# A spectral filter and a SoLU feed-forward layer on one core: the first entry's spectrum by channel halves, and its filter's sums on TensorE

## The chip, the cores and the metric

The kernel runs on one core of one Trainium2 chip. The metric is the device time of one execution in microseconds (us), the median over the runs. One more execution is recorded by the hardware profiler; its rows, groups and timelines are called the profile and the trace here.

Names: TensorE is PE (its weight loads PEld), VectorE is DVE, ScalarE is ACT, GpSimd is POOL, SyncE is SP. SP, ACT and POOL also issue DMAs, each on a queue of its own. A line such as L605 is line 605 of the kernel before.

## The reference

```python
X = np.fft.rfft(x, axis=1)                    # x: 8 entries, 3136 tokens, 256 channels, float32
Y = X * (filt_r + 1j * filt_i)[None, :, :]    # 1569 frequencies, 256 channels
y = np.fft.irfft(Y, n=3136, axis=1)           # bridge: (8 * 3136, 256) = 25088 tokens
h = y @ w_in                                  # w_in: 256 x 1024
e = np.exp(h - h.max(-1)); sm = e / (e.sum(-1) + 1e-9)
solu = h * sm
ln = (solu - mean(solu)) / sqrt(var(solu) + 1e-6) * g_ln
out = ln @ w_out                              # w_out: 1024 x 256
```

The weights lie in DRAM as 64-bit floats and are brought to 32 bits on the chip.

## The kernel before

Each entry's transform over 3136 = 49 x 64 tokens is done in two matrix products each way. The first step (`pa`) multiplies 49 rows by a table of 25 residues; the second (`pb`, in `forward`) multiplies, for each of 13 pairs of residues, two blocks of 64 rows by tables of cosines and sines and gives the spectrum, real part in one PSUM bank and imaginary part in another. The filter multiplies the spectrum; `inverse` (`pc`) goes back through the transposed tables; `back` (`py`) makes the tokens, which lie in `y` with channels on the partitions.

Entries 1 to 7 pass through DRAM between the steps (`d1`, `d2`) and are woven into a long loop over blocks of 128 tokens (`step`), which does the feed-forward layer: `product` (the `m` tiles), the maximum, exponential and mean, a turn by 32 x 32 blocks, `project` (the `o` tiles). Products are done by Strassen's scheme with 7 products for 8. Each step's place is written in lists; all orders on all engines are fixed when the program is built.

Entry 0 is done before the loop, in the opening, and stays on the chip. The change lies there. The opening's order is the order of the statements (`manual_schedule`), for each engine:

- x's 98 rows are fetched in 8 pieces of 4 + 4 columns (plain and mirrored); row 49 (the last of each half) comes apart, in four parts of 16 columns (`fetch_last`). The mirrored half of piece 0 and the four parts are issued by ACT, all else by SP. Then follow, on SP, tables and filters in three groups, half of w_in, constants, pieces of entry 1 and w_out.
- Each DMA of SP and ACT raises one of eight completion counters when it lands. The build hands the counters out in turn, and a DMA that gets a counter waits for the counter's earlier holder.
- VectorE brings two of the four raw quarters of w_in to 32 bits (`load_float64`, 9 instructions each).
- TensorE does 6 products that only warm it (`warm`), then `pa` (L605), which ACT evacuates (the last half piece VectorE); then rows of products that only keep it busy (`idle`) and the transposed tables (`tables_back`, L509).
- VectorE turns all of `pairs_x` in four quarters of 64 channels (`turn_rows`, L625), in place.
- Seven units of two pairs (the last has one, with one residue), 256 channels each: `forward` (8 products of 64 x 64 by 256 columns), four products with the filter on VectorE (L341, L342), a difference and a sum on POOL (L343), `inverse` (8 products), two evacuations on ACT (L359).
- `turn_rows` again; then the first step of three pieces of entry 1 (L245) with their stores, the other conversions, the sums of w_in's quarters, and `back` for all 8 pieces and both halves of the channels (L413).

PSUM has eight banks. Six of them, `ps_h`, go round in three pairs; two, `ps_t`, serve `pc`, the tables and `py`.

Of the kernel before, what the change touches and what calls it, by code (L numbers as in the profile page):

```python
# [9 lines left out]
FP32 = mybir.dt.float32  # L10
# [40 lines left out]
SHRINK = 1.0 / (32 * DFF)  # L51

# [51 lines left out]
def kernel(  # L104
# [327 lines left out]
    with ExitStack() as st:  # L432
        fpool = pool("fp", 1, stack=st)
        pools = {name: pool(name + "0", bufs, stack=st)
                 for name, bufs in (("r", 1), ("p", 3))}
        rows_x = pools["r"].tile([P, NH, C], FP32, name="x_0", tag="r")
        pairs_x = rows_x.rearrange("p m c -> p (m c)").rearrange("p (a c t) -> p a c t", c=C, t=2)
        wpool = pool("wp", 4, stack=st)
        ps_h = pool("ps_h", 3, PSUM, stack=st)

        def load_float64(dst, raw, power):


            lo, hi = raw[:, :, 0], raw[:, :, 1]
            frac, rest = dst.bitcast(I32), lo.bitcast(FP32)
            ts, tt, stt = (nc.vector.tensor_scalar, nc.vector.tensor_tensor,
                           nc.vector.scalar_tensor_tensor)
            return [
                lambda: ts(out=lo, in0=lo, scalar1=8, scalar2=None, op0=ALU.logical_shift_right),
                lambda: ts(out=power, in0=hi, scalar1=20, scalar2=0x7FF, op0=ALU.logical_shift_right,  # L450
                           op1=ALU.bitwise_and),
                lambda: ts(out=power, in0=power, scalar1=896.0, scalar2=0.0, op0=ALU.subtract,
                           op1=ALU.max),
                lambda: ts(out=power, in0=power, scalar1=255.0, scalar2=2.0 ** 23, op0=ALU.min,
                           op1=ALU.mult),
                lambda: ts(out=frac, in0=hi, scalar1=0xFFFFF, scalar2=3, op0=ALU.bitwise_and,
                           op1=ALU.logical_shift_left),
                lambda: stt(out=power, in0=hi, scalar=-2 ** 31, in1=power, op0=ALU.bitwise_and,
                            op1=ALU.bitwise_xor),
                lambda: tt(out=frac, in0=frac, in1=power, op=ALU.bitwise_or),  # L460
                lambda: stt(out=rest, in0=lo, scalar=2.0 ** -44, in1=power.bitcast(FP32), op0=ALU.mult,
                            op1=ALU.mult),
                lambda: tt(out=dst, in0=dst, in1=rest, op=ALU.add)]
# [6 lines left out]

        filters, tables = {}, {}


# [8 lines left out]
        def fetch_second(rows):  # L482
            for i in rows:
                second.fetch_x(i, [lambda out, in_: nc.sync.dma_start(out=out, in_=in_)] * 2,
                               spare_piece(i))

# [13 lines left out]
        one = fpool.tile([P, P], FP32, name="one", tag="one")  # L500

        def tables_back(i0, n):

            de = tables[i0][0]
            for first in range(0, n, 4):
                size = min(4, n - first)
                ps = ps_t.tile([P, 4, P], FP32, name=f"back_{i0}_{first}", tag="t")
                for v in range(size):
                    nc.tensor.matmul(out=ps[:, v], lhsT=de[:, first + v, 0].rearrange("p u q -> p (u q)"),  # L509
                                     rhs=one, start=True, stop=True)  # L510
                nc.scalar.copy(out=de[:, first:first + size, 1].rearrange("p i u q -> p i (u q)"),
                               in_=ps[:, 0:size])

# [5 lines left out]

        def resident(held):  # L520
            def find(sp, u):
                i, pairs = sp.units[u]
                tile, at = held[i]
                return tile[:, at:at + pairs]
            return find

        sp = Spectrum(0, pools, resident(filters), resident(tables))
# [6 lines left out]
        def halves(name):  # L534
            ps = ps_h.tile([P, 2, 512], FP32, name=name, tag="h")
            return [ps[:, u, :].rearrange("p (v c) -> p v c", c=C) for u in range(2)]

        def fetch_x(h, n0, n, r0, rows, dma):

            first, step = (n0, C) if h == 0 else (N2 - 1 - n0, -C)  # L540
            to = NR - 1 if r0 else (N1 - 1) * h
            dma(out=rows_x[to:to + rows, n0:n0 + n],
                in_=bass.AP(tensor=x.tensor, offset=x[0].offset + r0 * N2 * C + first * C,
                            ap=[[N2 * C, rows], [step, n], [1, C]]))
# [5 lines left out]
        def fetch_last(h, n0, dma):  # L550

            n = NH // 2
            first = n0 if h == 0 else N2 - n0 - n
            dma(out=rows_x[NR - 1 - h:NR - h, n0:n0 + n][:, ::1 - 2 * h],
                in_=bass.AP(tensor=x.tensor, offset=x[0].offset + ((N1 - 1) * N2 + first) * C,
                            ap=[[N2 * C, 1], [C, n], [1, C]]))

        for i in range(pieces):
            if i:
                fetch_x(0, NCH * i, NCH, 0, N1 - 1, nc.sync.dma_start)  # L560
            fetch_x(1, NCH * i, NCH, 0, N1 - 1, nc.sync.dma_start if i else nc.scalar.dma_start)
            if i == 0:
                fetch_last(1, 0, nc.scalar.dma_start)
                fetch_x(0, 0, NCH, 0, N1 - 1, nc.sync.dma_start)
                for h, n0 in ((0, 0), (0, NH // 2), (1, NH // 2)):
                    fetch_last(h, n0, nc.scalar.dma_start)
            if i in (2, 5):
                begin((0, 2)[i // 3], nc.sync.dma_start)
        nc.scalar.copy(out=small_consts[:, 5:6], in_=small_consts[:, 0:1])
        nc.gpsimd.dma_start(out=one, in_=one_dram)  # L570
        for i0, n in ((0, 4), (4, 4), (8, NP - 8)):
            for load in (load_tables, load_filters):
                load(i0, n, nc.sync.dma_start)
        begin(1, nc.sync.dma_start)
        begin(3, nc.sync.dma_start)
        nc.sync.dma_start(out=wf_t, in_=wf_dram)
        nc.sync.dma_start(out=wi_t, in_=wi_dram)
        nc.sync.dma_start(out=g_sb, in_=moe_g_ln.rearrange("(k p) -> p k", p=P))
        fetch_second(range(EARLY))
# [19 lines left out]
        for j in range(6):  # L599
            nc.tensor.matmul(out=ps_t.tile([P, P], FP32, name=f"warm_{j}", tag="t"), lhsT=wf0_t, rhs=wf0_t,  # L600
                             start=True, stop=True)
# [12 lines left out]
        def idle(out):  # L614

            nc.tensor.matmul(out=out, lhsT=one, rhs=one, start=True, stop=True)

        def idle_row(count, name):
            for j in range(count):
                idle(ps_h.tile([P, P], FP32, name=f"{name}_{j}", tag="h"))  # L620

        def turn_rows():
            for first in range(0, C, 64):
                part = pairs_x[:, :, first:first + 64].rearrange("p a c t -> p c a t")
                nc.vector.transpose(out=part, in_=part)  # L625

        for i0, n in ((0, 4), (4, 4)):
            idle_row(12, f"idle_{i0}")
            tables_back(i0, n)
        turn_rows()  # L630

        def start(i):
            i0, n = sp.units[i]
            sp.t2s[i] = pairs_x[:, i0:i0 + n]
            sp.fetch_filter(i)
            sp.fetch_de(i)
            sp.forward(i, halves(f"pb_0_{i}"))

        units = len(sp.units)

        order = [*range(units // 2), units - 1, *range(units // 2, units - 1)]
        for i in order[:2]:
            start(i)
        tables_back(8, NP - 8)
        early_weights = [op for ops in zip(conversion(1), conversion(3)) for op in ops]
        for at, i in enumerate(order):
            if at + 2 < units:
                start(order[at + 2])
            ended = at == units - 1
            sp.multiply(i, 0, nc.gpsimd.tensor_tensor)  # L650
            sp.multiply(i, 1, (nc.vector if ended else nc.gpsimd).tensor_tensor)
            if ended:
                for op in early_weights[:5]:
                    op()
            pss = [ps_t.tile([P, 2, C], FP32, name=f"pc_0_{i}_{u}", tag="t") for u in range(2)]
            i0, n = sp.units[i]
            sp.inverse(i, pss, pairs_x[:, i0:i0 + n], ended)
        turn_rows()
        for i in range(EARLY):
            for u in range(2):  # L660
                second.first(i, (u,), ps_t.tile([P, 2, C], FP32, name=f"pa_1_{i}_{u}", tag="t").rearrange(
                    "p a c -> p (a c)").rearrange("p (o n) -> p o n", o=1), nc.scalar.copy,
                    second.xs[i][0:NK, 2 * u:2 * u + 2, :])
                second.store_first(i, 2 * u, nc.gpsimd.dma_start)
        for ch in range(pieces):
            t4s[0, ch] = pairs_x[:, 2 * ch:2 * ch + 2]
        for op in early_weights[5:]:
            op()
        weight_sums(w_in_sb)
        for cb in range(KD):  # L670
            for ch in range(pieces):
                back(0, ch, cb, nc.scalar.copy)
# [557 lines left out]
```

## Time and profile before

| what | value |
|---|---|
| runs | 1584.10, 1579.68, 1583.47 us; median 1583.47 |
| span of the profiled execution | 1578.8 us |
| PE busy in the span | 1537.3 us (97%) |
| DVE, ACT, POOL busy | 1261.8, 923.8, 1142.2 us |
| granted TensorE clock, mean | 0.995 |
| first `pa`, first `pb`, first `py`, first `m` | 9.05, 36.75, 63.54, 78.67 us |

The profiled execution's own time is given as its span, from the first to the last instruction; what lies around the span is not in it. The last row is the start of each stage of the opening on TensorE. In the timelines a row gives start, duration, engine, line and operation, written tile and read tiles, count, and the idle time before it with what ended it. ACTq and SPq are DMA issues on these engines' queues. TensorE does a float32 product in two passes, and the trace counts passes.

### The profile page before, as it was taken

Reading aid. Unit: us, or ns where it says so; the run is one execution under the profiler, and the core shown is the slowest. Engines: PE = TensorE matmul, PEld = TensorE weight load, DVE = VectorE, ACT = ScalarE, POOL = GpSimd, SP = SyncE. Lnnn points to the kernel's source line nnn. Section 1 sums busy time; section 2 is a strip of 40 time slices with the busy share of each in tenths; the row PEclk is TensorE's granted clock in tenths of the full one; section 3 lists DMA queues with packets and bytes.
Section 4 is the critical chain, followed back from the end, with each engine's and each line's share of the span. In section 5 each row is a group of like instructions: output and inputs, shape, how many; then the busy total and the mean of one; then the engine's idle time right before and its main releaser. Section 6 shows DMA issues by size and latency. Waiting matters only on the chain. (4 is left out here: it accounts for less than half of the span.)

```text
span 1578.8 us, 36696 instructions
## 1 busy us (share of the span) xinstructions
PE 1537.3 (97%) x12836; PEld 1062.9 (67%) x12836; DVE 1261.8 (80%) x2280; ACT 923.8 (59%) x1886; POOL 1142.2 (72%) x1327
## 2 busy tenths in 40 slices
PE   7988999999999999999999999999999999999997
PEld 4733666667666776667666776667677777777777
DVE  4978978997989788877988688977997777777773
ACT  2455665566556556665556656566556665666562
POOL 0447976787878677887779767886766767676665
PEclk9999999999999999999999999999999999999999
DMA  9758877877987688667886588766874545344444
GB/s 248 229 162 228 241 211 209 244 207 202 242 260 206 174 231 250 205 172 189 240 234 195 151 227 240 215 179 174 228 207 120 139 123 132 90 115 109 108 111 106
DMA packets 341756, 298.08 MB, mean 189 GB/s; under 512 B 28096, under 2 KB 311370, under 8 KB 341572
## 3 DMA queue, kind: packets, MB, share of 16 engines
q1 hardware_dynamic: 276898, 172.78, 41.3%
q0 software_dynamic: 30352, 89.66, 18.9%
q10 hardware_dynamic: 34324, 33.30, 7.2%
q8 instruction: 104, 1.70, 0.5%
q14 instruction: 78, 0.64, 0.1%
HBM read 118.02 MB, written 74.84 MB: 122 GB/s over the span
## 5 line engine op out<-in xcount | busy, mean ns | idle before, releaser
L937 PEld LDWEIGHTS o<-w_out_sb,solu_t 128*128 128x128 f32 x3136 | 382.0, 192 | 49.2 <-issue 43.5
L801 PE MATMUL m<-w_in_sb,s 128*128 128x512 f32 x784 | 398.8, 610 | 6.5 <-DVE nmax L825 4.3
L937 PE MATMUL o<-w_out_sb,solu_t 128*128 128x128 f32 x3136 | 401.3, 276 | 2.7 <-DVE ot L957 2.3
L937 PEld LDWEIGHTS o<-w_out_sb,u 128*128 128x128 f32 x2352 | 307.3, 192 | 138.5 <-issue 107.1
L801 PE MATMUL m<-w_in_sb,y 128*128 128x512 f32 x588 | 308.2, 607 | 5.6 <-DVE nmax L825 4.1
L937 PE MATMUL o<-w_out_sb,u 128*128 128x128 f32 x2352 | 310.7, 276 | 2.5 <-POOL u L780 1.9
L847 DVE SCALAR_TENSOR_TENSOR h<-e,h 128x1024 f32<-128x1024 f32 x196 | 306.8, 1565 | 0.0
L811 ACT COPY h<-m 128x512 f32<-128x512 f32 x294 | 173.2, 589 | 198.6 <-PE m L801 179.8
L953 ACT ACTIVATE ot<-o,rs_t 128x128 f32<-128x128 f32 x392 | 143.5, 367 | 246.9 <-PE o L937 244.6
L780 POOL TENSOR_TENSOR u<-solu_t 128x512 f32<-128x512 f32 x98 | 133.7, 1365 | 187.2 <-DMA solu_t<-turn 108.8
L825 DVE CUSTOM_DVE_ANT_0 h<-m,h 128x512 f32<-128x512 f32 x196 | 134.0, 684 | 166.1 <-ACT h L811 101.8
L855 ACT ACTIVATE h<-h,nmu 128x1024 f32<-128x1024 f32 x196 | 225.0, 1148 | 56.4 <-DVE turn L865 56.4
L865 DVE STREAM_TRANSPOSE turn<-h 128x1024 f32<-128x1024 f32 x196 | 243.1, 1240 | 3.5 <-DMA out_dram<-ot 0.3
L835 ACT ACTIVATE e<-h,nmax 128x1024 f32<-128x1024 f32 x196 | 225.3, 1150 | 9.6 <-DVE h L847 8.2
L780 POOL TENSOR_TENSOR u<-solu_t,u 128x512 f32<-128x512 f32 x98 | 137.9, 1408 | 93.3 <-PE o L937 92.8
L801 PEld LDWEIGHTS m<-w_in_sb,s 128*128 128x128 f32 x784 | 128.1, 191 | 92.8 <-issue 71.9
L957 DVE SCALAR_TENSOR_TENSOR ot<-o,rs_t,ot 128x128 f32<-128x128 f32 x299 | 103.7, 347 | 99.9 <-ACT ot L953 58.0
L780 POOL TENSOR_TENSOR u<-u,solu_t 128x512 f32<-128x512 f32 x98 | 162.2, 1655 | 15.3 <-PE o L937 7.1
L801 PEld LDWEIGHTS m<-w_in_sb,y 128*128 128x128 f32 x588 | 96.7, 191 | 101.9 <-issue 48.4
L780 POOL TENSOR_TENSOR solu_t<-solu_t,solu_t 128x512 f32<-128x512 f32 x98 | 155.3, 1585 | 0.9
L780 POOL TENSOR_TENSOR s<-y 128x128 f32<-128x128 f32 x196 | 103.7, 529 | 14.7 <-ACT y L417 14.3
L390 PEld LDWEIGHTS py<-wb_t,t 50*64 50x64 f32 x3584 | 57.8, 134 | 43.8 <-issue 17.9
(122 smaller groups left out, 1942.5 us busy)
## 6 DMA issues: line engine op xcount, KB each, us to landing
solu_t<-turn SPq DMA_DIRECT2D x780, 128.0 KB
out_dram<-ot SPq DMA_DIRECT2D x196, 128.0 KB
t<-d POOLq DMA_DIRECT2D x112, 200.0 KB, 6.6
d<-x POOLq DMA_DIRECT2D x100, 200.0 KB, 5.1
f<-f_dram POOLq DMA_DIRECT2D x39, 512.0 KB, 7.8
t<-d ACTq DMA_DIRECT2D x37, 512.0 KB
d<-g POOLq DMA_DIRECT2D x36, 512.0 KB, 5.2
x<-in_x_dram SPq DMA_DIRECT2D x112, 98.0 KB
```

Of the source, the lines that this page charges most:

```text
L390: nc.tensor.matmul(out=views[g][64 * h:64 * h + 64, cb, i, :], lhsT=t4[rows, i, c0:c0 + 64], rhs=wb_t[rows, 0:N1], start=True, stop=True)
L780: nc.gpsimd.tensor_tensor(out=out, in0=in0, in1=in1, op=op)
L801: nc.tensor.matmul(out=ms[j, bank], lhsT=lhsT, rhs=w_in_sb[:, w, :], start=m in (1, 2, 7), stop=True, skip_group_check=True)
L811: nc.scalar.copy(out=h_half(k, i), in_=ms[j, 0])
L825: nc.vector.tensor_tensor_reduce(out=h_half(k, i), in0=ms[j, bank], in1=h_half(*kept), scale=1.0, scalar=sofar, op0=ALU.add, op1=ALU.min, ...
L835: nc.scalar.activation(out=e, in_=hs[k], func=AFT.Exp, bias=nmaxs.pop(k)[:, 1:2], scale=-1.0, accum_out=esums[g][:, i:i + 1])
L847: nc.vector.scalar_tensor_tensor(out=solu, in0=e, scalar=SHRINK, in1=solu, op0=ALU.mult, op1=ALU.mult, accum_out=nmu)
L855: nc.scalar.activation(out=solu, in_=solu, func=AFT.Square, bias=nmu, scale=-float(DFF), accum_out=variances[g][:, i:i + 1])
L865: nc.vector.transpose(out=turns[g][:, :, i, :], in_=solus[k].rearrange("p (f j) -> p f j", j=32))
L937: nc.tensor.matmul(out=pos[p, bank], lhsT=lhs[:, f, :], rhs=w[:, f, :], start=f == 0 and (m in (1, 2, 7) or alone), stop=True, skip_group_ ...
L953: nc.scalar.activation(out=out_half(p, *to)[0], in_=pos[p, 0], func=AFT.Copy, scale=rs)
L957: nc.vector.scalar_tensor_tensor(out=ot, in0=pos[p, bank], scalar=rs, in1=out_half(p, *kept)[0], op0=ALU.mult, op1=ALU.add)
```

## The change

It replaces the second half of entry 0's opening.

- The last row of x comes in two whole transfers of 32 columns, issued by ACT ahead of all others; ACT's third transfer is the mirrored half of piece 0.
- The second DMA order: the pieces of entry 1 now stand before the other half of w_in.
- A conversion to 32 bits takes 8 instructions.
- 8 warm-up products for 6; 12 idle ones for 24, with one group of transposed tables between them and two groups placed later.
- Units have four pairs (the last one pair, one residue) and one half of the channels, eight in all. The turn is done by quarters: two before the first `forward`, the others between units; the turn back likewise.
- `multiply` forms four products and no sum: those of the real part on VectorE; those of the imaginary part on POOL from a copy (`held`) that ACT makes, for five units, and on VectorE for three.
- `inverse` adds the products on TensorE: for each pair, residue and part it does one matrix product with the table and one with the table or its negative (`minus`, made by ACT next to the transposed tables).
- Each of the three pieces of entry 1 is done whole, one between units of the second half, one after the next turn, one at the end; they use a `ps_h` pair.

```diff
-        for i in range(pieces):
-            if i:
-                fetch_x(0, NCH * i, NCH, 0, N1 - 1, nc.sync.dma_start)
-            fetch_x(1, NCH * i, NCH, 0, N1 - 1, nc.sync.dma_start if i else nc.scalar.dma_start)
-            if i == 0:
-                fetch_last(1, 0, nc.scalar.dma_start)
-                fetch_x(0, 0, NCH, 0, N1 - 1, nc.sync.dma_start)
-                for h, n0 in ((0, 0), (0, NH // 2), (1, NH // 2)):
-                    fetch_last(h, n0, nc.scalar.dma_start)
+        for h in range(2):
+            fetch_last(h, nc.scalar.dma_start)
+        for i in range(pieces):
+            fetch_x(0, NCH * i, NCH, nc.sync.dma_start)
+            fetch_x(1, NCH * i, NCH, nc.sync.dma_start if i else nc.scalar.dma_start)
...
+        nc.sync.dma_start(out=wf_t, in_=wf_dram)
+        fetch_second(range(EARLY))
         begin(1, nc.sync.dma_start)
         begin(3, nc.sync.dma_start)
-        nc.sync.dma_start(out=wf_t, in_=wf_dram)
...
-        for j in range(6):
+        for j in range(WARM):
...
+                nc.scalar.mul(minus[:, i0 + first:i0 + first + size], ps[:, 0:size, 0:NQ], -1.0)
...
+        def multiply(k, half, shared):
+            i0, n, residues = extent(k)
+            rows = slice(0, NQ * residues)
+            f, at = filters[i0]
+            f = f[rows, at:at + n, :, P * half:P * half + P]
+            re, im = (ps[rows, 0:n] for ps in spectra.pop((k, half)))
+            parts[k, half] = of_re, of_im = [
+                ppool.tile([P, 2, 4, P], FP32, name=f"p{kind}_0_{k}_{half}", tag=f"p{kind}") for kind in "ri"]
+            for part in range(2):
+                nc.vector.tensor_tensor(out=of_re[rows, part, 0:n], in0=re, in1=f[:, :, part], op=ALU.mult)
+            if shared:
+                held = ppool.tile([P, 4, P], FP32, name=f"im_0_{k}_{half}", tag="im", bufs=1)[rows, 0:n]
+                nc.scalar.copy(out=held, in_=im)
+            engine = nc.gpsimd if shared else nc.vector
+            for part in range(2):
+                engine.tensor_tensor(out=of_im[rows, part, 0:n], in0=held if shared else im,
+                                     in1=f[:, :, 1 - part], op=ALU.mult)
+
+        def inverse(k, half):
...
+            for r in range(2):
+                for u in range(residues):
+                    rows = slice(NQ * u, NQ * u + NQ)
+                    for v in range(n):
+                        there = de[rows, at + v, 1, r, :]
+                        for part, by in ((of_re, there), (of_im, there if r else minus[rows, i0 + v, :])):
+                            nc.tensor.matmul(out=pss[u][NQ * r:NQ * r + NQ, v, :], lhsT=by,
+                                             rhs=part[rows, r, v], start=part is of_re, stop=True,
+                                             skip_group_check=True)
+            for u in range(residues):
+                nc.scalar.copy(out=pairs_x[:, i0:i0 + n, P * half:P * half + P, u], in_=pss[u][:, 0:n])
...
+        idle_row(6, "idle_0")
+        tables_back(0, 4)
+        idle_row(6, "idle_1")
+        for n in range(2):
+            turn_quarter(n)
+        forward(0, 0)
+        turn_quarter(2)
+        forward(1, 0)
+        multiply(0, 0, True)
+        tables_back(4, 4)
+        inverse(0, 0)
+        turn_quarter(3)
+        multiply(1, 0, True)
+        forward(0, 1)
+        inverse(1, 0)
+        multiply(0, 1, False)
+        forward(2, 0)
+        tables_back(8, NP - 8)
+        inverse(0, 1)
+        forward(3, 0)
+        multiply(2, 0, True)
+        forward(1, 1)
+        multiply(3, 0, False)
+        inverse(2, 0)
+        inverse(3, 0)
+        multiply(1, 1, True)
+        forward(2, 1)
+        turn_quarter(0)
+        first_of_second(0)
+        inverse(1, 1)
+        multiply(2, 1, True)
+        forward(3, 1)
+        turn_quarter(1)
+        first_of_second(1)
+        multiply(3, 1, False)
+        inverse(2, 1)
+        inverse(3, 1)
+        first_of_second(2)
+        for n in range(2, 4):
+            turn_quarter(n)
+        for j in (1, 3):
+            for op in conversion(j):
+                op()
```

## Prediction

> **What bounds the kernel now.** I read the page first: span, the busy rows, the chain.
>
> ```profile
> span 1578.8 us, 36696 instructions
> PE   7988999999999999999999999999999999999997
> DVE  4978978997989788877988688977997777777773
> ```
>
> From about 160 us on TensorE is at 9 tenths or more in nearly every slice, and the change leaves that part alone. An edit to the opening therefore shifts the end by what it shifts the moment at which TensorE takes up the long loop. The next view is the table by stretches, cut at the borders of the opening's stages (columns: stretch, PE, PEld, DVE, ACT, POOL busy, granted clock, DMA share, GB/s).
>
> ```profile
> 9.00:26.00 17.00, 16.95 (x32) 7.42 (x33) 9.09 (x18) 9.02 (x9) 0.00 (x0) 1.00 1.01 251
> 26.00:37.00 11.00, 7.99 (x69) 7.62 (x71) 9.58 (x5) 1.79 (x3) 0.00 (x0) 0.96 1.01 283
> 37.00:58.00 21.00, 18.06 (x210) 12.76 (x206) 19.13 (x36) 7.31 (x14) 15.03 (x13) 0.94 0.76 219
> 58.00:79.00 21.00, 20.81 (x141) 16.97 (x142) 20.89 (x35) 11.08 (x23) 3.33 (x6) 1.00 0.66 235
> 79.00:112.00 33.00, 25.34 (x52) 8.60 (x50) 26.51 (x82) 18.20 (x41) 17.83 (x28) 0.95 0.55 166
> ```
>
> TensorE holds 9 to 26, VectorE's turn 26 to 37, VectorE's filter products 37 to 58 (19.13 of 21 us), TensorE again 58 to 79. The timeline of PE gives the borders, and that of the ACT and SP queues what opens the first:
>
> ```profile
> 9.05 17.25 PE L605 MATMUL pa<-x,wf_t 98*128 98x512 f32 x32 [3.25 <-DMA x<-in_x_dram]
> 36.75 3.36 PE L320 MATMUL pb<-x,de 64*64 64x256 f32 x32 [3.01 <-DVE x L625]
> 63.54 15.30 PE L413 MATMUL py<-wi_t,x 128*128 128x98 f32 x128
> 78.67 1.91 PE L801 MATMUL m<-w_in_sb,y 128*128 128x512 f32 x4
> ...
> 0.74 0.42 ACTq L542 DMA_DIRECT2D x<-in_x_dram  x1
> 1.19 11.15 ACTq L554 DMA_DIRECT2D x<-in_x_dram  x4
> 3.52 0.50 ACTq L554 DMA_DIRECT2D x<-in_x_dram  x1
> 11.78 0.56 ACTq L554 DMA_DIRECT2D x<-in_x_dram  x1
> 14.15 0.32 SPq L542 DMA_DIRECT2D x<-in_x_dram  x1
> ```
>
> `pa` starts at 9.05 because the 16 KB piece of x's last row issued at 3.52 lands only then: 5.5 us for a small transfer while SP's queue is full. The four pieces take ACT's queue until 12.34, since each DMA waits for the earlier holder of its completion counter (eight, in rotation over both queues). The prices are the groups of 36 to 58 us and of the first 36:
>
> ```profile
> L342 DVE TENSOR_TENSOR pt<-pb,f 128x512 f32<-128x512 f32 x12 | 8.2, 682 | 0.0
> L343 POOL TENSOR_TENSOR pr<-pr,pt 128x512 f32<-128x512 f32 x6 | 7.7, 1282 | 38.2 <-DVE pt L342 38.2
> L359 ACT COPY x<-pc 128x512 f32<-128x512 f32 x11 | 6.3, 624 | 9.1 <-PE pc L320 7.1 <-issue 2.0
> L625 DVE STREAM_TRANSPOSE x<-x 128x2048 f32<-128x2048 f32 x4 | 8.9, 2280 | 0.0
> ```
>
> Start to start these are 0.60 (DVE product), 1.24 (POOL), 0.57 (ACT copy), 2.22 us (turn of a quarter).
>
> **The change, part by part.** *Loads of x.* Two whole transfers of the last row go first on ACT's queue, then the mirrored half of piece 0 (rows 48 to 95). The build hands out the counters in the order of its own plan, and there that third ACT transfer gets the counter that x's plain half of piece 1 and then of piece 4 hold: it waits until piece 4 has landed. In the trace of before, the DMA at 14.15 (piece 6) waits for that same piece 4, so piece 4 lands at 14.1; with 192 KB less ahead at 251 GB/s (0.8 us) I take 13.0 (12 to 14). From issue to landing: 5.5 us (the row at 3.52) at most, 3 us at least (the first transfer at 0.74, on empty queues, frees the counter for the 3.52 row, 2.8 us); I take 5, since SP's queue is as full then. So `pa` starts at 18.0 (15 to 20), not 9.05. DMA: Bandwidth & Descriptors, Queues, rings and completion order, of the Trainium skill says that each DMA engine takes turns between the rings of different queues; by that rule ACT's lone transfer would pass SP's backlog and land about 3 us after issue, making the sum 2 us less. The 5.5 us row speaks against it, and I keep the row.
>
> `pa` is 32 passes of 0.43 us at full clock, 13.8 us; the trace ran the first 8 at 0.86. TensorE will have idled since its 8 warm-up products ended near 6.4, so again half speed for 3.4 to 6.8 us, +2.5 (the two more warm-ups buy nothing). `pa` ends at 34.3 against 26.3, and with its last copy (1.0) and two turned quarters instead of four (4.44) the first forward transform starts at T = 39.7, against 36.75. So +3.0 although half the turn is off the path: that half is worth 4.4, and the late transfer costs it all and more. VectorE's shorter float conversion (8 instructions for 9, some 0.6 us each) lies under TensorE here.
>
> *The spectrum stage.* Before, VectorE alone set its length: 36.75 to 63.54, 26.8 us including the second turn and the pieces of entry 1. After, 10 of 24 large products go to POOL, from a copy of the imaginary part that ACT makes, POOL's 13 sums go, and TensorE sums in the inverse: 32 products of 128 columns for 8 of 256. Per large unit that is 64 passes, 16 in each quarter of the array; at 0.112 us a pass (the idle rows: 24 passes in 2.84) a quarter's run takes 1.8 us. I count the four quarters as concurrent, as the `pb` rows are (16 passes of 256 columns in 1.18 us). What I find decisive is ACT's order: the held copy of the next unit stands behind the two copies of this unit's inverse, and these behind POOL's second product. One shared unit is thus a ring: copy 0.6, two POOL products 2.48, inverse after the second one 1.8 + 0.3 to its last pass's end, two copies 1.14, four handovers of 0.05 to 0.07: 6.5 us. Counted from T, in the order of the program (unit and half), the copies behind each inverse end at: 0 first 7.8 (two more quarters, 4.44, pass VectorE meanwhile), 1 first 14.3, 0 second 20.2 (not shared, but the third tables are turned ahead of it in the same two PSUM banks), 2 first 26.7, 3 first 27.8 (small), 1 second 34.3, 2 second 40.8, 3 second 41.9, and entry 1's third piece at 43.5. Then `py`: stage 43.6 us against 26.8, +16.8. VectorE's own work in it is only 25 us (14 products 8.4, 8 small ones 2.6, six quarters 13.3, scale 0.6); it waits. Entry 1's three pieces and two of the four turned-back quarters are hidden in it; they are inside the 43.6.
>
> *Behind it.* `py` 15.3 us stays. Turns 3 and 4 (4.4), conversions 1 and 3 (2 x 3.8) and the sums (1.8) end on VectorE at T + 55.9 = 95.6, `py` at 98.6: TensorE stays the later. In the ramp from 94.8 to 107 VectorE runs without a gap on two conversions of w_out; 8 for 9 steps saves 0.65 each, -1.3. The clock may halve in gaps of the stage, as in the rows 26 to 37 and 37 to 58 (0.96 and 0.94: half speed from 36.1 to 39.5, after 3.4 us with 1.06 us of work); one inverse at half speed costs 1.8: I add +1.2 (0 to 5).
>
> **Sum:** +3.0 + 16.8 - 1.3 + 1.2 = +19.7. The profiled execution has a span of 1578.8, 4.7 under the median 1583.47 and 0.9 under the fastest run; the shift is the same on either. 1583.5 + 19.7 = **1603**.
>
> **Rivals.** *The runs of the inverse follow one another.* A quarter's 16 passes stand in one block; `pb` shows only blocks of 4 starting together (four within 0.04 us). If TensorE sees no further than one block, each large inverse takes 7.2 us instead of 1.8 after the second product: the stage becomes 70, the time 1629; two at a time gives +5.5, 1609. For it: no row shows longer blocks. Against: units wait anyway between the first and the second POOL product, in which half the runs can go. TensorE: Matmul & The Clock Gate, in its table and Architectural detail, of the Trainium skill gives the queue a depth of 64 with a partial reorder window; that would hold two such blocks with their weight loads, so the 1609 case. Chance 0.13.
>
> *The mirrored half of piece 0 is not late* (it lands by 6.4). Then `pa` runs from 6.4 with the clock up at 9 to 12 and is held by x's last pieces near 19.5, ends at 21.4 to 23, T = 27.7, and `py` starts at 71.3: +7.8, after the other terms 1591. Against it: the order of counters in the program, which for before agrees with every wait of the trace. Chance 0.13.
>
> *Faster:* the early T = 27.7, and VectorE rather than the ring of ACT, POOL and TensorE sets the stage. Its 25 us of work plus one unit's tail let `py` start at 54 instead of 63.5: 1574. It decides for a gain once the stage is under 35.8 us. For it: POOL and ACT are free most of this time in total (12.4 and some 16 us of work). Against: both conditions are needed, and the orders on ACT and POOL are fixed. Chance 0.06. *No change* (the stage at 35 to 40 us with early x): 0.04.
>
> **How the numbers follow.** Forecast 0.64, rivals 0.13, 0.13, 0.06, 0.04. The forecast's own bounds are 1592 to 1614: the transfer (-3 to +2, more if the clock comes late), the clock (-1 to +4), handovers of 11 dependent steps (-5 to +5). To reach 8 in 10 the low end goes to 1588 (most of the early-transfer case), the high end to 1616 (two runs at a time). This kernel can tell 0.3%, 4.8 us, from no change. Faster 0.07, same 0.04, slower 0.89.
>
> **What would show it.** In the profile after: `pa`'s first row starts at 15 to 20, released by a DMA of x, with an ACT queue row of x near 13; the first `pb` near 40; POOL's pairs of products 6.5 us apart, with POOL idle until ACT's copy, and ACT idle until `pc`; `py` starts near 83, the first `m` near 99. Wrong in the first step if `pa` starts before 9; wrong in the second if POOL's pairs follow at under 4.5 us, or VectorE shows no idle time between its products; the first rival is right if the `pc` passes of one unit spread over more than 5 us. If these hold and the end still moves by under 10 us, the ramp gave it back: then idle time between 100 and 130 us of the old kernel would be missing in the new one.

## The result, and the profile after

The changed kernel takes 1622.58 us (median of 4 runs, 1617.52 to 1630.18); the kernel before, run beside it, 1582.24 us. The ratio is 1.0258, with a 95% interval of 1.0227 to 1.0289: slower by 40 us, where the prediction had 20 and a range that ended at 1616.

The page of the changed kernel, the lines that answer to those of before:

```profile
span 1620.5 us, 37453 instructions
PE   5898899999999999999999999999999999999997
DVE  2467997888898879986889779886898777777773
```

From the sixth slice on TensorE stands at 9 tenths, as before; the first three slices of VectorE fell from 4, 9, 7 to 2, 4, 6. The table by stretches, cut at the borders of before (columns as there):

```profile
9.00:26.00 17.00, 2.24 (x3) 1.17 (x4) 8.05 (x16) 1.47 (x2) 0.00 (x0) 1.00 1.03 246
26.00:37.00 11.00, 11.00 (x23) 4.69 (x22) 0.00 (x0) 5.38 (x5) 0.00 (x0) 1.00 0.96 271
37.00:58.00 21.00, 18.27 (x202) 15.61 (x204) 12.07 (x9) 5.88 (x10) 2.51 (x2) 0.92 0.81 232
58.00:79.00 21.00, 17.11 (x240) 16.25 (x234) 4.65 (x10) 5.04 (x11) 4.97 (x4) 1.00 0.55 199
79.00:112.00 33.00, 32.73 (x324) 28.11 (x321) 17.76 (x26) 12.43 (x22) 6.62 (x7) 1.00 0.12 38
```

TensorE works 2.24 us between 9 and 26, where it was full before; from 58 to 79, in the middle of the new spectrum stage, VectorE works 4.65 of 21 us, ACT 5.04 and POOL 4.97. Only TensorE is busy there for most of the time, 17.11 us: ACT and VectorE wait for its products, and POOL for ACT's held copy. The timeline of PE gives the new borders, that of ACT's queue what opened the first:

```profile
23.76 16.73 PE L590 MATMUL pa<-x,wf_t 98*128 98x512 f32 x32 [15.69 <-DMA f<-in_filt_r_dram]
46.55 3.54 PE L626 MATMUL pb<-x,de 64*64 64x128 f32 x64 [2.29 <-DVE x L606]
102.78 15.21 PE L417 MATMUL py<-wi_t,x 128*128 128x98 f32 x128
117.82 1.91 PE L852 MATMUL m<-w_in_sb,y 128*128 128x512 f32 x4
...
0.74 4.56 ACTq L543 DMA_DIRECT2D x<-in_x_dram  x2
14.99 0.36 ACTq L531 DMA_DIRECT2D x<-in_x_dram  x1
```

ACT's third transfer, the mirrored half of x's piece 0, is issued at 14.99, and `pa` starts at 23.76. (The name in the brackets is the DMA that landed last by the profile; `pa` does not read `f`. What it waits for is the transfer of 14.99, as the experiment that issues it first shows.) The first `pb` comes 9.8 us later than before, the stage from there to `py` takes 56.2 us instead of 26.8, and the first `m` is 39.2 us late. From the first `m` to the end of the span it is 1502.7 us against 1500.1.

How TensorE spends the stage is seen best in the second half of unit 0, whose four products were all ready long before. PE's timeline, the start of its 64 inverse passes (64 x 64 each, 16 in each quarter of the array):

```profile
69.14 0.43 PE L661 MATMUL pc<-pr,de 64*64 64x128 f32 x2 [0.74 <-ACT y L514]
69.41 0.38 PE L661 MATMUL pc<-pi,y 64*64 64x128 f32 x2
69.63 0.38 PE L661 MATMUL pc<-pr,de 64*64 64x128 f32 x2
...
70.28 0.38 PE L661 MATMUL pc<-pi,y 64*64 64x128 f32 x2
70.50 0.43 PE L661 MATMUL pc<-pr,de 64*64 64x128 f32 x4
70.72 0.43 PE L661 MATMUL pc<-pi,y 64*64 64x128 f32 x4
71.00 0.38 PE L661 MATMUL pc<-pr,de 64*64 64x128 f32 x2
...
74.93 0.27 PE L661 MATMUL pc<-pi,de 64*64 64x128 f32 x1
```

One product (two passes) starts every 0.22 us. Twelve passes of the first quarter go alone; only at 70.50 and 70.72 do the rows hold four passes, the last two products of this quarter beside the first two of the next. Then the second quarter goes alone from 71.00. The unit takes 6.1 us, 69.14 to 75.20, with one quarter of the array at work nearly all the time.

### The profile page after: what moved, and what is told of

Read it like the earlier page. It is cut to its first block, busy times and chain, and to the rows that moved or that the text cites. A ratio compares the mean times of both kernels' runs of the same rounds, so it can differ in the third digit from the quotient of the medians.

```text
span 1620.5 us, 37453 instructions
## 1 busy us (share of the span) xinstructions
PE 1563.0 (96%) x13216; PEld 1090.3 (67%) x13216; DVE 1258.5 (78%) x2260; ACT 927.6 (57%) x1894; POOL 1138.7 (70%) x1321
## 4 chain that ended last, share of the span: by engine, by line
PE 63%; DMA 4%; DVE 1%; POOL 1%; issue 1%; SPq 0%; ACTq 0%; DVEq 0%; POOLq 0%; ACT 0%
PE o L988 28%; PE m L852 28%; PE py L394 3%; PE pa L292 2%; DMA solu_t<-turn 2%; PE pb L324 2%; PE pc L324 2%; DMA de<-de_tbl 1%; DMA x<-in_x_dram 1%; DMA out_dram<-ot 1%; POOL x L283 0%; PE o L952 0%; SPq L933 0%; DVE h L898 0%; DVE pr L347 0%
## 5 line engine op out<-in xcount | busy, mean ns | idle before, releaser
L988 PEld LDWEIGHTS o<-w_out_sb,solu_t 128*128 128x128 f32 x3136 | 382.1, 192 | 47.9 <-issue 43.6
L831 POOL TENSOR_TENSOR u<-u,solu_t 128x512 f32<-128x512 f32 x98 | 158.4, 1616 | 15.9 <-PE o L988 7.7
L831 POOL TENSOR_TENSOR s<-y 128x128 f32<-128x128 f32 x196 | 105.1, 536 | 14.3 <-DVE power L458 13.8
L394 PEld LDWEIGHTS py<-wb_t,t 50*64 50x64 f32 x3584 | 57.8, 134 | 43.5 <-issue 19.4
```

The costliest lines, as they stand in the source:

```text
L394: nc.tensor.matmul(out=views[g][64 * h:64 * h + 64, cb, i, :], lhsT=t4[rows, i, c0:c0 + 64], rhs=wb_t[rows, 0:N1], start=True, stop=True)
L831: nc.gpsimd.tensor_tensor(out=out, in0=in0, in1=in1, op=op)
L988: nc.tensor.matmul(out=pos[p, bank], lhsT=lhs[:, f, :], rhs=w[:, f, :], start=f == 0 and (m in (1, 2, 7) or alone), stop=True, skip_group_ ...
```

## The experiments

The stages below are read from PE's timeline of the one profiled execution of each kernel: the first `pb`, the first `py`, the first `m`. The rest, from the first `m` to the end of the span, lies between 1494.9 and 1504.4 us in all kernels. Each ratio is taken against the kernel before as it ran beside the kernel in question; its medians there lay between 1578.9 and 1582.2 us, so kernels are better compared by their ratios than by their medians.

| kernel | first pb | stage to py | first m | median, us | ratio to before (95%) |
|---|---|---|---|---|---|
| before | 36.75 | 26.8 | 78.67 | 1582.2 | 1 |
| changed | 46.55 | 56.2 | 117.82 | 1622.6 | 1.0258 (1.0227 to 1.0289) |
| early x | 31.97 | 67.0 | 113.99 | 1611.2 | 1.0180 (1.0138 to 1.0223) |
| early x, again | 32.23 | 56.2 | 103.49 | 1610.5 | 1.0175 (1.0144 to 1.0207) |
| four quarters | 46.75 | 45.6 | 107.42 | 1607.2 | 1.0165 (1.0136 to 1.0194) |
| two quarters | 47.70 | 45.3 | 108.06 | 1608.0 | 1.0176 (1.0150 to 1.0202) |
| early x, two quarters | 31.96 | 46.7 | 93.68 | 1595.4 | 1.0095 (1.0065 to 1.0125) |
| the same, products on VectorE | 31.39 | 39.7 | 86.12 | 1589.1 | 1.0052 (1.0032 to 1.0073) |
| early x, two quarters, copy ahead | 30.61 | 43.5 | 89.15 | 1591.2 | 1.0067 (1.0044 to 1.0090) |
| VectorE, four quarters | 30.38 | 36.6 | 82.04 | 1583.9 | 1.0018 (0.9995 to 1.0040) |
| copy ahead, four quarters | 32.79 | 35.6 | 83.39 | 1585.6 | 1.0029 (1.0015 to 1.0043) |
| copy ahead, four quarters, VectorE | 31.97 | 37.7 | 84.76 | 1586.5 | 1.0038 (1.0021 to 1.0054) |
| VectorE, four quarters, tables and pieces early | 30.76 | 31.8 | 77.66 | 1582.9 | 1.0014 (0.9997 to 1.0032) |

The theory after the result had two parts: the late transfer costs the start some 15 us, and the block order of the inverse's products some 10 us of the stage. The main rival was that the order of ACT, POOL and TensorE around the held copy (the prediction's ring) is longer than computed.

**Early x.** The first transfers of x are issued so that ACT's wait for no completion counter:

```diff
+        fetch_x(1, 0, NCH, nc.scalar.dma_start)
         for h in range(2):
-            fetch_last(h, nc.scalar.dma_start)
+            fetch_last(h, (nc.scalar if h == 0 else nc.sync).dma_start)
         for i in range(pieces):
             fetch_x(0, NCH * i, NCH, nc.sync.dma_start)
-            fetch_x(1, NCH * i, NCH, nc.sync.dma_start if i else nc.scalar.dma_start)
+            if i:
+                fetch_x(1, NCH * i, NCH, nc.sync.dma_start)
```

> The changed kernel, but ACT issues the mirrored half of x's piece 0 first and one transfer of the last row second; SP issues the other one behind its first table, so that none of these waits for a completion counter. Nothing else is changed. Theory: the late transfer costs the start of pa 15 to 17 us. Then pa starts at 6 to 9 instead of 23.76, the first pb at 29 to 32 instead of 46.55, the spectrum stage stays at 56 us, and the time is 1606 to 1608 (-15). Rival: x's last pieces, the filters or a half clock take the place of the wait; then pa starts early and the first pb still comes after 38, or the stage grows, and the time stays above 1614.

`pa` started at 7.54 and the first `pb` at 31.97, as the theory had it. But the stage grew to 67.0 us, so that the first `m` came only 3.8 us earlier, and the median, 1611.2, is neither the 1606 to 1608 of the theory nor above the 1614 of its rival. The table by stretches of this kernel, and of the same kernel when it was run and profiled again:

> The kernel with the early loads of x alone once more, to see whether its long stage is a matter of chance. There TensorE's clock was at half from 46 to 60 and from 70 to 81, in the runs of one-quarter blocks, where other kernels lost 3.4 us at a time. Theory: a clock that drops in such a run stays down until something denser comes, and whether it drops depends on where the pauses fall; so stage and time scatter: single times between 1600 and 1616, stage 56 to 67. Rival: it is fixed by the order of the work: stage 66 to 68 again and all times above 1608.

```profile
46.00:60.00 14.00, 14.00 (x103) 13.50 (x101) 1.84 (x3) 1.49 (x3) 0.81 (x1) 0.52 0.79 229
...
70.00:81.00 11.00, 11.00 (x98) 10.82 (x97) 2.08 (x3) 2.00 (x4) 0.42 (x2) 0.53 0.10 38
```

```profile
46.00:60.00 14.00, 13.25 (x162) 12.88 (x163) 2.21 (x4) 2.86 (x7) 1.18 (x1) 1.00 0.79 232
...
70.00:81.00 11.00, 10.73 (x87) 7.34 (x81) 6.87 (x10) 4.15 (x7) 4.57 (x5) 1.00 0.22 77
```

The third number from the end is the granted clock: 0.52 and 0.53 in the first profile, 1.00 in the second. In the second the stage is 56.2 us, as in the changed kernel, and the first `m` at 103.49: the early transfer is worth 14.3 us at the first `pb`, and all of it reaches the first `m`. By the medians it is 11 to 12 us. Its single times lay between 1600.2 and 1615.5, those of the first run between 1600.8 and 1615.8; the two executions with the highest mean clock (0.997 and 0.996) took 1600.8 and 1600.2, the two with the lowest (0.988) 1615.8 and 1615.5. So the long stage is not fixed by the order of the work, and it goes with the clock: 23.9 us at half speed can cost up to 12 us of TensorE's time, and the stage was 10.8 us longer. What made the clock fall in one execution and not in the other stays open.

**Order of the inverse's products.** Two kernels with the loads of the changed kernel, and only the loops of the inverse in another order, first four quarters, then two:

```diff
-            for r in range(2):
-                for u in range(residues):
-                    rows = slice(NQ * u, NQ * u + NQ)
-                    for v in range(n):
+            for v in range(n):
+                for r in range(2):
+                    for u in range(residues):
+                        rows = slice(NQ * u, NQ * u + NQ)
```

```diff
             for r in range(2):
-                for u in range(residues):
-                    rows = slice(NQ * u, NQ * u + NQ)
-                    for v in range(n):
+                for v in range(n):
+                    for u in range(residues):
+                        rows = slice(NQ * u, NQ * u + NQ)
```

> The changed kernel, but the loops of the inverse run over pairs first, so that its products go round the four quarters of the array; all of them now stand behind POOL's second product. Theory: 16 passes in one block keep the other quarters waiting; in turns the 64 passes of a large unit take 2.2 to 2.6 us (the forward's 32 take 1.1) instead of 5.5 to 6.8, the stage falls from 56.4 to about 46 (six large units, 1.7 each), the time to 1611 to 1613. Rival: the quarters share something else (a PSUM bank, the weight loads), the passes still take 5 us or more, now all behind the second product: stage 57 to 70, time 1623 to 1636.

> The changed kernel, but inside each half of the inverse (first POOL product, second POOL product) the products alternate between two quarters. Theory: each half takes 1.8 to 2.2 us instead of 3 to 3.5, and the first half still lies under POOL's second product: POOL's pairs 6.5 to 6.8 us apart instead of 8.4, stage 44 to 45 as the prediction had it, time 1609 to 1612. Rival (the order of the blocks is of no account): pairs stay 8.4 apart, time 1620 to 1624.

The stage fell to 45.6 and 45.3 us, by 10.6 and 10.9, and the first `m` by 10.4 and 9.8; the times are a little under the ones expected. The second half of unit 0 took 6.1 us in blocks, 3.7 us by two quarters (66.11 to 69.78) and 2.4 us by four (66.97 to 69.33). In the kernel with two quarters PE's timeline shows a product starting every 0.22 us in each of two quarters; here from the second part of that unit:

```profile
68.26 0.43 PE L661 MATMUL pc<-pr,de 64*64 64x128 f32 x4
68.47 0.43 PE L661 MATMUL pc<-pi,de 64*64 64x128 f32 x4
68.69 0.43 PE L661 MATMUL pc<-pr,de 64*64 64x128 f32 x4
68.91 0.43 PE L661 MATMUL pc<-pi,de 64*64 64x128 f32 x4
```

POOL's pairs of products, first of the changed kernel, then of the one with two quarters:

```profile
50.64 2.51 POOL L647 TENSOR_TENSOR pi<-im,f 128x512 f32<-128x512 f32 x2 [48.63 <-DMA raw_out<-in_moe_w_out_dram]
59.02 2.49 POOL L647 TENSOR_TENSOR pi<-im,f 128x512 f32<-128x512 f32 x2 [5.87 <-ACT im L644]
...
85.44 2.50 POOL L647 TENSOR_TENSOR pi<-im,f 128x512 f32<-128x512 f32 x2 [6.56 <-ACT im L644]
93.82 2.49 POOL L647 TENSOR_TENSOR pi<-im,f 128x512 f32<-128x512 f32 x2 [5.32 <-ACT im L644]
```

```profile
71.44 2.49 POOL L647 TENSOR_TENSOR pi<-im,f 128x512 f32<-128x512 f32 x2 [10.50 <-ACT im L644]
78.36 2.51 POOL L647 TENSOR_TENSOR pi<-im,f 128x512 f32<-128x512 f32 x2 [4.44 <-ACT im L644]
85.29 2.49 POOL L647 TENSOR_TENSOR pi<-im,f 128x512 f32<-128x512 f32 x2 [3.07 <-ACT im L644]
```

8.4 us apart in the changed kernel, 6.9 with two quarters. POOL waits for the held copy in both. The rivals of both expectations (the order is of no account, or the quarters share something else) are out. That four quarters are no better than two here has a reason in the order: all 64 passes then stand behind POOL's second product, while with two quarters 32 of them lie beside it. The clock has a part in it too. In the profile with four quarters it was at half for three stretches of 3.4 us, each during a large inverse (from 53.1, 59.9 and 73.6); with two quarters it was at half once, ahead of the first inverse. POOL's first two pairs with four quarters, 50.73 and 58.30, are 7.6 us apart with a half clock between them, its last two, at the full clock, only 6.0:

```profile
78.99 2.51 POOL L647 TENSOR_TENSOR pi<-im,f 128x512 f32<-128x512 f32 x2 [5.53 <-ACT im L644]
85.02 2.48 POOL L647 TENSOR_TENSOR pi<-im,f 128x512 f32<-128x512 f32 x2 [2.19 <-ACT im L644]
```

By these rows four quarters make the shorter ring at the full clock (6.0 against 6.9), and their stage would be under 45.6 us; by how much was not measured.

**Both edits** (early x, two quarters):

> The changed kernel with both edits: early loads of x, and the inverse's products alternating between two quarters. Theory: the two losses add up and nothing else of size is left out of the prediction's arithmetic. First pb at 32, stage 45 to 47, py at 78, first m at 93 to 94, time 1596 to 1600. Rival: with the early start TensorE's clock halves in the stage as it did with the early loads alone (0.50 from 48 to 56 and 72 to 80, the stage 67 instead of 56); then the stage is 50 to 56 and the time 1602 to 1610, and the early start is worth little by itself.

The first `pb` at 31.96, the stage 46.7, the first `m` at 93.68, 24.1 us earlier than in the changed kernel: 14.3 and 9.8 add up. The median is 1595.4, 27 us below the changed kernel's (26 by the ratios). The clock was lost for 3.4 us in this profile's stage (at half from 37.4 to 40.8). What is left against before is 15.0 us at the first `m`.

**What makes up the rest of the stage.** First, all products on VectorE (`multiply(..., False)` for all units), then the same with four quarters:

> As the kernel with both edits, but all four products of every unit on VectorE: no held copy, no product on POOL. Theory: what remains of the stage is the ring of ACT's copy, POOL's two products, the inverse and ACT's two copies; without it VectorE's own work sets the stage (25 us + 10 products of 0.6 = 31, and 4 to 6 us of tail): 35 to 38 instead of 46, time 1586 to 1590. Rival: TensorE's inverse and the copies behind it set it whoever multiplies: stage 44 or more, time as with both edits.

> As the kernel with all products on VectorE, but the inverse goes round all four quarters instead of two. Its products are ready 0.6 us apart, so nothing is gained by waiting for the first half. Theory: of the 39.7 us of its stage the six large inverses take 3.6 each; at 2.0 each the stage is 30 to 33, the first m at 77 to 79, the time 1580 to 1583. Rival: TensorE then idles more and its clock halves, as in the kernel with four quarters and POOL (0.75 to 0.82 in the stage): stage 36 to 40, time 1586 to 1590.

Without the held copy and POOL's products the stage is 39.7 us instead of 46.7, 7 us less, of which the clock, at its full speed throughout this stage, can be up to 1.7. So the ring was a limit; but the stage is 2 us longer than the theory's upper end. With four quarters, which have no second POOL product to wait for, it is 36.6 and the first `m` comes at 82.04. That step was expected at 7 to 10 us and brought 3.1 to 4.1. The clock was not the reason in the way the rival had it: it was at half for 3.4 us at the very start of the stage only. What took the rest of the step is not shown by these two kernels.

Second, the order on ACT. The products of the next unit are put ahead of the inverse of this one, in the whole list:

```diff
         multiply(0, 0, True)
         tables_back(4, 4)
-        inverse(0, 0)
         turn_quarter(3)
         multiply(1, 0, True)
         forward(0, 1)
-        inverse(1, 0)
+        inverse(0, 0)
         multiply(0, 1, False)
         forward(2, 0)
+        inverse(1, 0)
...
-                held = ppool.tile(..., tag="im", bufs=1)[rows, 0:n]
+                held = ppool.tile(..., tag="im", bufs=2)[rows, 0:n]
```

> As the kernel with both edits, but the products of the next unit stand ahead of the inverse of this one (a second buffer for the held copy), so that ACT makes the held copy before it evacuates; entry 1's pieces stand at the end. POOL keeps its products. Theory: the ring is only an order on ACT; POOL's 12.4 us and VectorE's 25 us overlap then, the pairs on POOL follow at 3 to 5 us, stage 32 to 38, time 1583 to 1590. Rival: POOL's pace or TensorE's inverse is the limit by itself: stage 43 or more, time 1594 or more.

> As the kernel with the held copy ahead, but the inverse goes round all four quarters, and two of entry 1's pieces stand between the units again (at the end all three cost TensorE 5.4 us). Theory: what kept that kernel at 43.5 us was its inverse (3.5 to 4.5 us per unit, VectorE's products waiting for its operands' buffers); stage 31 to 36, first m 77 to 82, time 1580 to 1586. Rival: POOL's pair of products (2.5 us behind a copy of 0.6) is itself the limit, stage 40 or more, time over 1588.

> As that kernel, but all products on VectorE. VectorE's work in the stage is 25 us, TensorE's about 28. Theory: stage 29 to 33, first m 75 to 79, time 1577 to 1583, level with the kernel before the change or just ahead of it. Rival: two buffers for the products are too few, or the clock halves: stage 36 or more, time over 1586.

With two quarters and the copy ahead the stage was 43.5 us, as the rival gave it, and the time between the two. POOL's first two pairs followed at 3.3 us there, 34.70 and 38.02, so the ring was indeed broken; what was late next was the inverse. The pair of copies behind one inverse came 4.6 us after that of the one before (40.66, 45.26), and the `pr` products on VectorE waited for the inverse to give back the two buffers of its operands. Then entry 1's three pieces held TensorE for 5.4 us ahead of `py`. With four quarters and two pieces back between the units the stage was 35.6, within the theory's range; the first `m`, 83.39, came just after it. With all products on VectorE in this order it was 37.7; there the clock was at half from 37.6 to 44.4, and the theory's 29 to 33 was missed. So with four quarters the two cures (no POOL, or the copy ahead) are worth about the same, and they do not add: even without the 3.4 us that the half clock can have cost it, the kernel with both is at 34.3, close to either alone. Their stages are 9 to 10 us under the 45.6 of four quarters alone, but up to 5 us of that 45.6 can be the clock's (10.2 us at half).

Last, the third tables were loaded and turned ahead of the first inverse, and the three pieces of entry 1 put one behind each of the last three forward transforms:

> As the kernel with all products on VectorE and four quarters, but the third tables are loaded ahead of the second filters and turned next to the second tables, ahead of the first inverse, and entry 1's three pieces stand one behind each of the last three forward transforms, none at the end. Theory: the third tables cost the second half of unit 0 some 4 us in the two PSUM banks that the inverse uses, and the last piece 2 us ahead of py; the stage falls from 36.6 to 30 to 33, the first m from 82 to 76 to 79, the time to 1577 to 1581, level with or just under the kernel before the change. Rival: the pieces displace other work of TensorE and the filters come later; stage 35 or more, time 1582 or more.

The stage fell to 31.8 us and the first `m` to 77.66, 1.0 us earlier than before the change. The time is 1582.9, ratio 1.0014 (0.9997 to 1.0032): level with the kernel before, above the 1577 to 1581 that was expected. In the profile the lead of 1.0 us at the first `m` was gone by 85 us, in a wait for a sum on POOL (0.8 us) that the kernel before does not have there; waits for pieces of x (2.1 us together, 1.8 before) had TensorE 0.4 us behind at 92.6. A shorter wait for VectorE near 107 us (2.7 for 3.4) gave it a lead of 0.3 us again at `ps_mean` (114.75 against 115.03). No version that was run is measurably faster than the kernel before.

## Why the prediction was wrong

The sign was right, and both causes were named: the late transfer as a term, too small, and the blocks of the inverse as a rival, at nothing in the sum. Of the 39.2 us at the first `m` the prediction had 21.0 with its clock term (3.0 + 16.8 + 1.2); 18.2 were missing, some 6.9 ahead of the first `pb` and 11.4 in the stage behind it (56.2 for 43.6 + 1.2).

- **Loads of x: right mechanism, term mis-sized.** The third ACT transfer did wait for its counter. But it was issued at 14.99, not 13.0, and landed about 8.7 us after that, not 5, so that `pa` started at 23.76 instead of 18.0 (5.8 us) and the first `pb` at 46.55 instead of 39.7 (6.9 us, with 1.1 more between the two). The step that failed is the choice of the 5.5 us row as the upper end. That row is a piece of 16 KB; this transfer is 192 KB. By the view of DMA queues, ACT's queue moved no packet before 17 us, most from 17 to 20, and its last ones between 22 and 23. Size alone does not do it: the same 192 KB at 0.74 in the kernel before landed within 2.8 us, on nearly empty queues. Which part is the size and which SP's full queue no run separates. Issued early, the transfer let the first `pb` start at 31.97 and 32.23, where the second rival had 27.7. DMA: Bandwidth & Descriptors, Queues, rings and completion order, of the Trainium skill has the engines take turns between rings, from which the prediction worked out 3 us; the trace, with 8.7, is further from that than the prediction was.
- **The spectrum stage: the count of concurrent quarters failed.** "I count the four quarters as concurrent, as the `pb` rows are" took a row with short blocks for one with blocks of 16 passes. The quarters followed one another with an overlap of two products, and the passes of one unit spread over 6.1 us, the prediction's own sign for its first rival. That rival was right in its mechanism, which was given 0.13, and too dear in its price (a stage of 70): half of each run does lie beside POOL's second product, which its text had noted as the reason against it. The two experiments on the order give 10.6 and 10.9 of the 11.4 us.
- **The ring: right.** With two quarters in turns, which restores 1.8 us behind the second product, the pairs stand 6.9 us apart (6.5 computed) and the stage is 45.3 us (43.6 and 1.2 for the clock computed). With early x as well the stage is 46.7. That ACT's order makes the ring was right too: with the copy ahead POOL's first pairs follow at 3.3 us. The stage itself fell by 7.0 us without POOL and by only 3.2 with the copy ahead, where entry 1's pieces had moved to its end.
- **The clock: right in size in the changed kernel, by luck.** It was at half from 46.4 to 49.8 only, and not during an inverse, as the term has it, but during the first forward passes (64 in 3.54 us; 2.05 in the kernel with four quarters, at the full clock). The early-x kernel shows that the same stage could have lost 10.8 us; the bound of +5 was too low.
- **Behind it.** `py` took 15.0 us, and TensorE stayed the later, as computed. The -1.3 us from the shorter conversion can't be seen: from the first `m` to the end the changed kernel took 2.6 us more than before, and this stretch scatters by some 9 us over the kernels that were run (1494.9 to 1504.4). No run isolated it, so it stays open.
- **The range.** The high end of 1616 was set by two runs at a time, without the late transfer being any later. Both causes were on their dear side at once, and the range did not allow for that: 6.9 from the transfer alone reach 1610, and the blocks alone 1614.

## What to carry to other kernels

When small products are laid into quarters of the array, look at the order in which they are written: here the quarters work side by side only if neighbouring products go to different quarters, and a block of 16 passes in one quarter costs nearly its full length. Price a transfer by one of its own size that had the same traffic beside it: here neither the small one under a full queue nor the large one on nearly empty queues gave the time. And write the load that opens the first stage where no counter can hold it back. When work is handed from one engine to another and back, count the ring that each engine's fixed order makes, and undo it before counting the shares of busy time.

## What the runs showed of the hardware

Passes of 64 x 64 by 128 columns start 0.11 us apart in one quarter, and at the end of a block two of its products ran beside the first two of the next quarter (the rows at 70.50 and 70.72), as if TensorE looked that far ahead. TensorE: Matmul & The Clock Gate, Part 2: What happens when you issue a matmul, Step-by-step, of the Trainium skill says that "MATMULs themselves stay in program order" and only weight loads are pulled ahead. The traces agree, but for those two products: 6.1, 3.7 and 2.4 us for the same 64 passes in three orders.

The granted clock fell for 3.4 us at a time (once for 6.8) in most kernels, often around the first `pb`, ahead of which TensorE had been idle for 2.3 us (3.0 before the change); two kernels with the same 2.3 us kept the full clock through the stage. In the first profile of early x it stayed at half for 13.7 and 10.2 us although TensorE was busy for 14.00 of 14 and 11.00 of 11 us. Up to 55 and 78 us these stretches were blocks of one quarter; behind them came forward passes of the next unit, and in the first also the turned tables, until the clock was back at 60.1 and 80.6. TensorE: Matmul & The Clock Gate, Part 1: The HAM clock gate, of the Trainium skill has the clock return after one busy window of about 3.4 us. Here it did not, while with four quarters in turns it came back after 3.4 us three times. In the second profile the same blocks ran at 1.00 in the same stretches, so thin use of the array does not bring the clock down by itself. That it keeps a fallen clock down is argued from these two stretches; no run changed it alone.
